# A kernel of bucketed attention and a Mish feed-forward layer: a new table of order and engine behind the beginning of the program

## The chip, the cores and the metric

The kernel runs on one core of a Trainium2 chip. The metric is the device time of one execution in microseconds (us). A core has five engines that each work through their own instructions in order: TensorE (PE, with the weight loads PEld shown apart), VectorE (DVE), ScalarE (ACT), GpSimd (POOL) and SyncE (SP), which here issues the DMA transfers. An engine waits for another through semaphores.

## What is computed

Four batches of eight heads with 768 positions and 64 features go through attention that is masked by hash buckets; then 3072 tokens of 512 features go through a feed-forward layer with Mish, h x tanh(softplus(h)). Inputs are float32, the two weight matrices float64.

```python
q_bits = (np.einsum('bhsd,dk->bhsk', q, proj) > 0).astype(np.int64)
k_bits = (np.einsum('bhsd,dk->bhsk', k, proj) > 0).astype(np.int64)
...
mask = q_bucket[:, :, :, None] == k_bucket[:, :, None, :]
scores = scale * np.matmul(q, k.transpose(0, 1, 3, 2))
scores = np.where(mask, scores, -1000000000.0)
scores = scores - np.max(scores, axis=-1, keepdims=True)
attn = np.exp(scores)
attn = attn / (np.sum(attn, axis=-1, keepdims=True) + 1e-09)
return np.matmul(attn, v).astype(np.float32)
...
h = x @ w_in
sp = np.where(h > 20.0, h, np.log1p(np.exp(np.minimum(h, 20.0))))
g = h * np.tanh(sp)
return (g @ w_out).astype(np.float32)
```

## The kernel before

The function `lsh_attention_mish_ffn` does not issue work as it goes. It builds a plan of 2809 operations, numbered from 0 in the order of the algorithm. An operation (class `Plan`, method `op`) has a name, what it reads and writes, and one or more alternatives: an engine, an estimated duration and a function that issues its instructions. At the end `Plan.ordered` walks through the text `ORDER` and issues each operation where its number stands there. A letter behind the number takes an alternative other than the first (b the second, and so on). So the table fixes two things: the order of instructions on every engine, SP's transfers included, and, for operations with alternatives, the engine. Work is issued in that order under a manual schedule; the framework adds the semaphore waits that the order and the data need.

The program has these parts, all of which overlap in the table:

- *Preparation.* Weights arrive as float64 words and are joined to float32 by integer work (`w_u`, `w_sign`, `w_low`, `w_join`), measured by a sum of squares (`square` on ACT or `gram` on PE), scaled by a power of two and split into two float16 parts (`w_hi`, `w_lo`). q, k and v are split in the same manner. The power of two comes from `stat`: `st` (two small matmuls on PE into columns of the bank ps_t), `half` (DVE reads that), `pw` (DVE or POOL).
- *Attention front*, 96 steps, S0 to S95. A step is two heads by 128 queries. S is eight matmuls into ps_s (768 columns per head, of 512 and 256); from step 13 on there is only one ps_s, so that S waits for both exps of the step before. `max` (DVE, L870) reduces it, `scl` (L876 to L882; DVE in two forms, or POOL) makes the scale and bias, two `exp` (ACT, L895) write the buffer pb and the row sums.
- *Attention back.* `sums`, `rv` (L919), then for each head `hi` (float16 of p times 1/sum: ACT, POOL or DVE; L390, L388, L391), `lo` (what is left: DVE L406, or two instructions on POOL, L412 and L413) and a transposing DMA (`ptturn`, L423) into PT.
- *V*, 48 of them (L951, 36 matmuls each), writes half of the bank ps_t: even ones columns 0 to 255, odd ones columns 256 to 511, which `st` and the hash matmuls `hp` use too. `x_hi` (ACT, L957) and `x_lo` (DVE, L960) read it into X.
- *Feed-forward*, 96 steps. H (24 matmuls, L982 to L984) writes one of two banks, `mish` (ACT, L1000) reads it, `g_hi` and `g_lo` split the result, and O (six matmuls, L1020 to L1022, for each half s of the tokens) accumulates over g. `ob` (ACT or DVE) scales the sum, and a DMA stores it. H8 to H15 need the whole X of the second group of queries, that is V4 to V7.

Mish and exp need different tables on ACT, so that each change between them loads one (ACT_TABLE_LOAD).

The operations that the later text speaks of, with their numbers: S14 558, its max 559, scl 560 and exps 561, 562; S15 599 (scl 601), S16 641 (max 642, scl 643, exps 644, 645), S17 657; V6 646, V7 678; `st` 581, `half` 582, `pw` 583, `w_hi` 584 and 534; x_lo 648 and 680; `lo` 633 on POOL; O30 596; H8 689.

The lines that turn the table into a program, and the alternatives of `scl`:

```python
for w in ORDER.split():
    n, a = (int(w[:-1]), "abcd".index(w[-1])) if w[-1].isalpha() else (int(w), 0)
    o = self.ops[n]
    assert all(q in done for q in o.preds), o.name
    done.add(o)
    yield o.alts[a][2]
...
op("scl", [("DVE", 410, port(lambda: scale(nc.vector, both))), ("DVE", 515, lambda: scale(nc.vector, single)),
           ("POOL", 380, lambda: scale(nc.gpsimd, both))],
```

Of the kernel before, what the change touches and what calls it, by code (L numbers as in the profile page):

```python
# [87 lines left out]
185 14 1 0 71 3 15 107 7 5 6 13 72 42 73 74 134 4b 22 2 16 25 81 26 27 43b 17 76 23 45 8 78 44 77 82 9 48 10 11 24  # L88
12 18 46 49b 19 83 47 20 21 58b 31 84 50 88 51 33 59 85 86 52 87 53 60 108b 56 54 57 110 90 61 55 34 113 146c 109
111 79 126 114b 147b 112 75 89 35 91 115 32b 97 148b 116 123c 80 36 37 118 69 117 28 39 119 29 38 197b 125 124 121  # L90
40 30b 149 41 62 67b 129 63 122 68 92 120 65 93 64 130 94b 66 167 198b 135b 95 70 168 131c 150 136b 132 133 137 199b
98 180 138 159d 169c 160 96 161c 170 200 158 162 163 201 250b 165 164 139 171 251b 181 157 172c 232 209 144 252b 140
208 151 182c 142 166 202 152 210 145b 153 183 173 233 99 174 100 175 211 102 103 101 141 234c 176 186b 143 104 253
184 212 187c 224c 195b 154b 213 127 177 188 155b 214b 225 178 189 226 156 235 245 179 228 215b 196 261 236 229 355
217 190 279b 274 246 227 218 280b 305b 237d 191 105b 230 216 203 263 106 281b 231 193 204 192 238 275 205b 247c 239b
206b 194 240 241 219 254 248 128 276c 207 242 427 249 243 262 266c 306b 220 244 277 255 267 256 300 257 268 221 222
258b 282 223 307b 270 283 269 308 278 271 272b 301 309 292c 259b 329 316 293 310 294 311 302c 312 273 260 334b 318
296 303 317 335b 330 297 264 319 304 295b 320 313 321c 356 331c 298 336b 265 299 314 332 284 322 428 285 286 337 323
290 291 388b 287b 315 338 288b 325 389b 357 326 333 324 383 347d 346 348 339 358c 349 327 390b 351 328 372 289 359
345 361b 352 391 360 362b 384 340 392 400 350 409 375d 363b 376 353 385c 393 377 354 364 414b 379 365 399 373 415b  # L100
341 386 410 380 394 387 378b 366 416b 374 452 401d 411c 395 381 402 417 382 367 403 457b 405 426 412 396b 368 458
# [12 lines left out]
740 707c 673 726 759c 674 676 675 709 677 757 760 724 761 710 785 792 783b 763b 762 725 906 786 779b 787b 764 708c
788 794 765 789 780 766 793 743 803b 1018 711 744 813 712 714 804 795 713 715 745 770 746 814 747b 748 798 805 771b
815c 907 750 772 816 767 807 818 751 801c 910 802 817 806c 819 834c 749 835 1017 808 784 768 845 1019 836 809 769
796b 812 838b 846 810 799 820 752 811 821 753 847b 755 754 839 849 797 842 837b 848 822 923 756 823 800 824 840 825b
865 856 911 827 868 908c 828 857 858b 924 851 869 841 914 873 859c 843 854b 870c 852 855 850 871 912 853 874 860 844
909 861 872 864 862 826 913 903 829 894c 918 863 875 866 895 830 876 896b 927 919 967 920 898 921 877 902 878 922
879 831 880c 944 889 832 882 897 833 946 936c 904 900b 937 899 938 931 947 925b 883 948 959 940 867 949 901 926 950  # L120
890 945 915 939c 941 951c 881c 932 942b 962 952 928 933 891 960 963 968 884 943 961 885 964 953c 965 969 981 970 955
916 982 887 956 917 954c 966 957 987d 958 999 983 985 984 988 971b 886 989 1020 888 934 1000 972b 990b 929b 1001b
991 1002 1024 930 992 1003 974 1021 1028 993 975 1012 1025 1029 1022 994 973 892b 1037 1004b 1204 1158 1005 1030b
# [24 lines left out]
1520b 1577b 1488 1562 1530 1586 1475 1521c 1587 1531 1494 1532 1578 1508 1523 1588 1476 1580 1477 1620 1589c 1533
1590 1550c 1571 1524 1600 1621 1623 1591 1622 1581 1563 1543 1601 1522b 1579 1652 1602b 1960 1593 1603 1564 1594
# [1027 lines left out]
```

## Time and profile before

| | |
|---|---|
| median of 3 runs | 849.79 us (849.61 to 850.22) |
| the profiled execution | 849.03 us, its span 847.3 us |
| PE, busy share of the span | 92% (779.9 us) |
| DVE | 79% (665.4 us) |
| ACT | 72% (612.8 us) |
| POOL | 29% (248.1 us) |
| DMA queue of the kernel, share of 16 engines | 84.8% |

The span runs from the first to the last instruction; the rest of the profiled time lies around it. Busy shares are averages over stages with different limits. In a row of a group stand line, engine, operation, out<-in with shapes and count, then busy us and mean ns of one, then the idle time of the engine just before them and what ended it. In a row of the timeline stand the start, the duration, the engine, the line, and in brackets the idle time before it with its releaser. In a row that gives one tile's instructions stand the shortest, median and longest duration in ns.

### The profile page before, as it was taken

How to read it: one execution, taken by the hardware profiler on the slowest of the kernel's cores; microseconds unless marked ns; L12 is line 12 of the kernel's file. 1: busy time of each engine (PE TensorE's matmuls, PEld its weight loads, DVE VectorE, ACT ScalarE, POOL GpSimd, SP SyncE). 2: the span in 40 equal slices, each digit the busy share in tenths (PEclk: the TensorE clock that was granted, in tenths of full speed). 3: DMA queues.
4: the chain of work that ended last, by engine and by line, in shares of the span. 5: the costliest groups of instructions: out<-in, count | busy, mean ns of one | idle time of the engine just before them, and what ended most of it. 6: DMA issues, size and time to landing. Idle time of an engine off the chain costs nothing. (4 is left out here: it accounts for less than half of the span.)

```text
span 847.3 us, 17219 instructions
## 1 busy us (share of the span) xinstructions
PE 779.9 (92%) x6630; PEld 537.1 (63%) x6630; DVE 665.4 (79%) x1292; ACT 612.8 (72%) x939; POOL 248.1 (29%) x289
## 2 busy tenths in 40 slices
PE   5555768899999999999999999999999999999998
PEld 4333545577667666666666676676677677666764
DVE  6979899888889898888798867789888877767311
ACT  6878899798778667667878867697778765577221
POOL 3546543313231420234311352221213223322000
PEclk9868699999999999999999999999999999999999
DMA  9899999699999978899998878999997785575300
GB/s 312 221 218 237 270 232 223 137 212 212 237 194 197 180 144 162 150 160 234 155 215 167 157 146 138 187 150 210 189 170 135 144 150 101 100 125 107 69 26 26
DMA packets 426547, 144.02 MB, mean 170 GB/s; under 512 B 395744, under 2 KB 416224, under 8 KB 426464
## 3 DMA queue, kind: packets, MB, share of 16 engines
q1 hardware_dynamic: 426464, 142.91, 84.8%
q8 instruction: 52, 0.85, 0.4%
q14 instruction: 31, 0.25, 0.1%
HBM read 36.70 MB, written 7.34 MB: 52 GB/s over the span
## 5 line engine op out<-in xcount | busy, mean ns | idle before, releaser
L895 ACT ACTIVATE pb<-ps_s,svb 128x768 f32<-128x768 f32 x192 | 188.7, 986 | 62.9 <-DVE svb L882 38.5
L982 PE MATMUL ps_acc<-X,wi 128*128 128x256 f16 x768 | 210.1, 274 | 0.5 <-ACT ffb L1000 0.5
L983 PE MATMUL ps_acc<-X,wi 128*128 128x256 f16 x768 | 210.0, 273 | 0.0
L984 PE MATMUL ps_acc<-X,wi 128*128 128x256 f16 x768 | 209.9, 273 | 0.0
L870 DVE TENSOR_REDUCE svb<-ps_s 128x2 f32<-128x1536 f32 x96 | 168.4, 1754 | 43.6 <-PE ps_s L864 41.1
L406 DVE SCALAR_TENSOR_TENSOR hl<-pb,svb,hl 128x768 f16<-128x768 f32 x161 | 164.9, 1030 | 12.7 <-ACT hl L390 8.3
L864 PE MATMUL ps_s<-KT,QT 128*128 128x512 f16 (+1 forms) x768 | 148.4, 338 | 21.1 <-ACT pb L895 16.0
L1022 PE MATMUL ps_o<-wo,ffb 128*128 128x512 f16 x384 | 145.5, 379 | 1.4 <-DVE ffb L406 1.4
L1020 PE MATMUL ps_o<-wo,ffb 128*128 128x512 f16 x384 | 145.6, 379 | 0.0
L1021 PE MATMUL ps_o<-wo,ffb 128*128 128x512 f16 x384 | 145.5, 379 | 0.0
L864 PEld LDWEIGHTS <-QT 128*128 128x128 f16 x768 | 75.1, 100 | 75.8 <-issue 30.4
L951 PE MATMUL ps_t<-PT,VT 128*64 128x256 f16 x1728 | 107.2, 281 | 2.8 <-DVE ho L477 2.0
L951 PEld LDWEIGHTS <-VT 128*64 128x64 f16 x1728 | 94.9, 113 | 17.2 <-issue 15.7
L390 ACT ACTIVATE hl<-pb,svb 128x768 f16<-128x768 f32 x83 | 76.4, 930 | 33.0 <-DMA PT<-hl 15.4
L406 DVE SCALAR_TENSOR_TENSOR ffb<-ffb,smalls 128x512 f16<-128x512 f32 x96 | 72.0, 758 | 35.0 <-POOL ffb L388 27.0
L983 PEld LDWEIGHTS <-wi 128*128 128x128 f16 x768 | 75.3, 98 | 14.9 <-issue 0.5
L982 PEld LDWEIGHTS <-wi 128*128 128x128 f16 x768 | 75.3, 98 | 13.4 <-issue 1.6
L388 POOL TENSOR_SCALAR hl<-pb,svb 128x768 f16<-128x768 f32 x45 | 43.2, 961 | 136.8 <-DVE svb L919 85.2
L984 PEld LDWEIGHTS <-wi 128*128 128x128 f16 x768 | 75.4, 98 | 9.0
L895 ACT ACT_TABLE_LOAD x43 | 55.2, 1283 | 34.2 <-DVE svb L880 20.4
L1000 ACT ACTIVATE ffb<-ps_acc,smalls 128x512 f32<-128x512 f32 x96 | 62.9, 684 | 21.8 <-PE ps_acc L984 15.5
L412 POOL TENSOR_SCALAR pb<-pb,svb 128x768 f32<-128x768 f32 x31 | 30.6, 987 | 138.5 <-ACT hl L390 56.9
(176 smaller groups left out, 990.0 us busy)
## 6 DMA issues: line engine op xcount, KB each, us to landing
out_dram<-ffb SPq DMA_DIRECT2D x24, 256.0 KB, 2.8
stg<-in_k_dram SPq DMA_DIRECT2D x12, 384.0 KB, 4.0
stg<-in_v_dram SPq DMA_DIRECT2D x12, 384.0 KB, 4.2
stg<-in_q_dram SPq DMA_DIRECT2D x9, 512.0 KB, 4.9
wi<-in_moe_w_in_dram SPq DMA_DIRECT2D x7, 512.0 KB, 4.7
wo<-in_moe_w_in_dram SPq DMA_DIRECT2D x6, 512.0 KB, 7.1
stg<-in_moe_w_out_dram SPq DMA_DIRECT2D x6, 512.0 KB, 4.4
PT<-hl SPq DMA_TRANSPOSE x192, 4.0
```

Of the source, the lines that this page charges most:

```text
L390: ACT=lambda: nc.scalar.activation(dst, src, AF.Copy, scale=sc),
L406: return [("DVE", 215 + 1.035 * n, port(lambda: nc.vector.scalar_tensor_tensor(out=dst, in0=src, scalar=sc, in1=hi, op0=ALU.mult, op1=ALU. ...
L864: nc.tensor.matmul(sc[:, hh * S + c0 * P:hh * S + c1 * P], QTb[:, u % 2, sl, qi], KTb[:, j, sl, hh * NCH + c0:hh * NCH + c1].rearrange("p ...
L870: op("max", [("DVE", 1790, lambda: nc.vector.tensor_reduce(out=sv[:, 0], in_=sc.rearrange("p (h e) -> p h e", h=2), axis=AX.X, op=ALU.max, ...
L895: EXP[n, hh] = op("exp", [("ACT", 1075, lambda hh=hh, t=t: nc.scalar.activation(pb[:, t], sc[:, hh * S:(hh + 1) * S], AF.Exp, bias=sv[:, 2 ...
L951: nc.tensor.matmul(pv[hh * D:(hh + 1) * D, 0:256], vt[:, w, hh * NCH + c], pt[:, hh, a * NCH + c].rearrange("p s t -> p (s t)"), start=(x ...
L982: nc.tensor.matmul(o, wh, X[:, 0, c], start=(c == 0), stop=False)
L983: nc.tensor.matmul(o, wh, X[:, 1, c], start=False, stop=False)
L984: nc.tensor.matmul(o, wl, X[:, 0, c], start=False, stop=(c == NCC - 1))
L1020: nc.tensor.matmul(PS[f"o{s}"], gh, wo[:, g, 0, f2], start=first, stop=False)
L1021: nc.tensor.matmul(PS[f"o{s}"], gh, wo[:, g, 1, f2], start=False, stop=False)
L1022: nc.tensor.matmul(PS[f"o{s}"], gl, wo[:, g, 0, f2], start=False, stop=last)
```

## The change

Only the text `ORDER` is replaced. The same 2809 numbers stand in it, in another order and partly with other letters. The first lines of the table differ only in how the engines' operations are interleaved. The rest of the source is unchanged. Of the diff these are the first lines, and those around the operations named above:

```diff
-185 14 1 0 71 3 15 107 7 5 6 13 72 42 73 74 134 4b 22 2 16 25 81 26 27 43b 17 76 23 45 8 78 44 77 82 9 48 10 11 24
+185 14 1 0 71 3 15 107 7 5 6 13 72 42 134 73 4b 22 2 74 25 81 26 27 43b 16 23 45 8 17 44 76 82 9 78 48 10 11 24 77
 12 18 46 49b 19 83 47 20 21 58b 31 84 50 88 51 33 59 85 86 52 87 53 60 108b 56 54 57 110 90 61 55 34 113 146c 109
...
-508 436 527b 477 513 490 523b 514 524 528c 525 515 437 481 483 529 558 538d 467 537 503 536 487 547 433c 484b 539
-516 563b 485 517 530 504 438 559 505b 551 488 506b 540b 541 564 560c 542 548 555 552 507 543 561 439 640 565c 440
-518 544 556 562 557 566 531 576b 599 586d 532 489 575 567 545 533b 587 577b 600 588 568 520 534 589 569 601b 519
-549b 590 602 592 591 603 535 629c 641 593 570b 630 550 571b 546 573 578b 572 594 631 579 574 491 595 632 633b 492
-642 580 553b 581 646 582 615b 635 634 643c 583 554 584b 636 604c 637 585 645 596 644 605 649 657 606c 650 607 651
-678 653b 658 614 608 647 679 648 652 680 659 654 609 689 610 638b 661 611b 612c 660 613 681c 697 690 619c 616b 620
...
+508 436 527b 477 513 490 523b 514 524 528c 525 437 515 481 483 529 558 538d 467 503 487 547 537 433c 484b 536 539
+640 516 563b 485 517 530 504 438 439 551 505b 559 488 548 540b 506b 564 541 560 555 542 552 561 565c 543 507 519 440
+489 562 566 556 599 586c 576b 557 575 544 531 567 532 587 545 600 533b 577b 588 568 546 549b 569 534c 589 518 601
+570b 590 602 592 591 603 535 571b 641 593 550 629c 578b 630 572 595 573 631 579 574 520 491 633b 642 580 632 581 594
+492 553b 582 643 583b 634 646 635 584b 554 645 636 585 644 637 604c 649c 615b 657 605 647 650 606c 651 648 678 607
+653b 658 614 608 596 679 680 659b 609 689 610 661 611 612c 660 613 619b 693 616 690 620 621c 622 617c 662 652 618
...
```

More of the change, by code (lines that the diff above doesn't have):

```diff
@@ L92 @@
[L92 to L101, printed above, removed]
+111 126 114b 147b 112 89 35 91 115 79 32b 97 148b 116 123c 36 37 118 75 117 28 39 119 29 38 197b 125 80 124 121 69
@@ L114 @@
[L114 to L123, printed above, removed]
@@ new lines @@
+1358 1342 1295 1322 1359 1377 1347c 1362 1389 1378 1379 1350 1273 1380b 1363 1312 1351 1390 1364b 1421 1365b 1349
+1391b 1304c 1392 1382 1343 1425 1367 1393 1383 1308b 1410d 1411 1305 1412 1309 1429 1368 1381 1414 1422 1442 1430
+1415 1426 1413c 1321 1366 1431 1445c 1433 1384 1434 1446 1385 1552 1423c 1432 1416 1353 1396 1417 1447d 1369 1397
+1457 1370 1371 1372 1448 1373 1450 1449b 1352 1458 1443 1463 1398 1438 1399 1459b 1400 1453 1401b 1460 1454 1403
+1374 1451 1462 1495 1402c 1452 1461 1424 1439 1478 1479 1404 1489 1496 1354 1490 1435 1498b 1605 1418 1491c 1480b
@@ new lines @@
+1787 1750c 1788 1778 1719 1777c 1779 1780b 1789 1767 1806 1819 1807 1808b 1809 1781 1810 1842 1820 1811b 1821 1812
+1822 1838 1751 1813 1823 1843 1824b 1825 1635 1814 1846 1801 1741 1815 1826 1768 1847 1839 1855 1754b 1848 1827c
+1849 1828 1755 1783 1829 1837 1850 1859 1992 1862b 1830 1863 1840c 1831 1864b 1872 1865 1851 1873 1874b 1866 1875
+1804 1867 1876 1782 1852 1877 1966 1841 1888 1878 1844c 1868 1784 1856 1889 1869 1967b 1894 1879 1890b 1860 1853b
+1881 1891 1816 1880c 1882 1854 1920 1802 1861 1803 1883 1892 1845 1895 1884 1897d 1969b 1817 1898 1906 1900 1899
@@ new lines @@
+1832 1907 1924 1857b 1908b 1901 1909 1858 1902 1910 1870 1903 1833 1904 1921 1929 1942 1930 1911c 1925 1912 1931
+1871 1913c 1932 1915 1934 1896 1916 1914c 1933 1917 1945c 1922b 1955 1946 1947b 1886 1970 1956 1948 1893 1918 1957b
+1949 1885 1958 1923 1950 1959 1887 1951 1943 1968 1926 2026 1971 1987 1976 1952 1972 1993 1977 1944 1973 1974 2007
+1978 1988 1834 1989b 1938 2008 1980 1990 2009 1981 1991 1935 1994 1905 1975 1995 1996 2010b 1997c 2021 2011 1999
+1979 1919 2012 1982 2000 1939 2022 2053 1983 1936c 2023b 2014 2024 2057 1927 2015 2013c 1937 2025 2237 1998c 1953
@@ new lines @@
+2016 2042c 2028 2017 2061 2054 1954 2062 2029 2001 2074 2058 2002 2043 2063b 2044c 2064 2045c 2030 1985 2031 2046
+2003 2032b 2004 2006 2047 2065 2077 2078 2079c 2075 1984 2005 2033c 2048 2089 2095 2035b 2080 2066 2082 2090 2049
+2081 2091b 2055 2036 2092 2070 2083 2056 2093 1818 2076 2084 1940b 2110b 2111 1986 1941 2094 2085 2067 2121 2112c
+2086 2114 2127 2071 2068 2122 2059b 2115 2180 2128 2123b 2130b 2129 2125 2131 2060 2037 2018 2113c 2116 2124 2050
+2117 2132c 2034 2133 2134c 2141 2051 2072 2038 2019b 2147 2096 2136b 2176 2142 2097 2143b 2137 2135c 2144 2087 2039
@@ new lines @@
+2269 2262 2270b 2272 2157 2288 2158 2200 2228 2271 2260c 2160 2285 2263 2239 2292 2264 2240 2159 2196 2241b 2289
+2229 2242c 2161 2273b 2293 2297 2274 2294c 2276 2275b 2286b 2279 2231 2295 2374 2277 2301 2244 2278 2296 2245 2243
+2308d 2230 2255 2309 2310 2287 2280 2318 2256b 2298 2251 2319 2302 2422 2265 2320b 2290c 2281 2321 2291 2467 2370
+2299c 2312 2303b 2311c 2322 2314 2282 2246 2323d 2305 2266 2324 2304 2325 2247 2166 2300 2423 2327b 2334 2313 2371
+2187 2317 2335 2315 2332 2328 2336c 2338 2424 2384 2425 2205 2426b 2326c 2248 2249 2329 2250 2337 2316 2427c 2306
@@ new lines @@
+2330 2307 2352 2468 2343b 2344 2346 2340 2353 2345 2354 2366 2347 2355 2349 2348 2356 2357b 2375 2358 2350 2367
+2359c 2361b 2331 2376 2341 2333 2372b 2342 2377c 2362 2351 2360b 2378 2363 2380 2429 2379 2368c 2430 2391d 2369 2339
+2381 2392 2394b 2364 2401 2397b 2385 2365 2428 2402 2382b 2388 2386 2403b 2393c 2404 2395 2399 2387 2396 2431 2405
+2400 2432 2398 2406b 2373 2417 2407 2408 2283 2437 2389 2418 2410b 2409 2419b 2414 2438 2420 2383 2411 2412 2415
+2421 2390 2440 2436 2441 2434 2439 2442 2451 2444b 2470 2452 2445 2453c 2454 2474 2413 2455 2471 2456b 2443c 2478
@@ new lines @@
+2446b 2475 2416 2479 2483 2433 2480 2469 2481 2457 2458c 2460 2487 2472c 2461 2482 2459c 2473 2484 2476c 2447 2462
+2504 2494c 2464 2488 2267 2505 2463 2552 2495 2506b 2477 2507 2496c 2498 2491 2497c 2465 2500 2508 2466 2448 2501
+2553 2509b 2510 2520 2499 2511 2556 2521 2492 2435 2513 2566 2560 2522b 2514 2512b 2449b 2523 2485 2515 2503 2489
+2516 2524 2502 2529b 2486 2530 2493 2538 2554b 2531c 2526 2539 2540b 2574 2533 2541 2532c 2534 2542 2535 2517 2543
+2536 2544 2490 2561 2545c 2567 2518 2562 2557 2519 2563 2546c 2564 2570 2547 2549 2548 2558c 2565 2555 2525 2550
@@ new lines @@
+2527 2587 2568c 2577b 2578 2579c 2537 2580 2588 2581b 2575 2551 2528 2589b 2585 2559 2582 2591 2576 2609 2590 2592d
+2583b 2603 2610 2571 2611 2600 2604 2639 2593 2605 2594c 2606 2596 2643 2595c 2597 2598 2607 2572c 2584 2612c 2569
+2640 2623 2613 2599 2586 2615 2624 2644 2652 2641c 2625b 2614c 2626 2573 2602 2616 2618 2617 2627 2601 2628 2629
+2619 2620 2630 2645c 2653 2632b 2647 2450 2656 2648 2631 2633 2634 2721 2649b 2635 2642 2650 2608 2651 2636 2657
+2663b 2621b 2664 2646 2673 2722 2695 2665 2674 2675 2660 2637b 2676 2666c 2667 2729 2668 2677 2678b 2669 2689 2679
@@ L205 @@
+2775 2785b 2788 2786 2777 2789 2790 2795 2793 2794 2796 2797 2799 2801 2798 2803b 2802 2804 2800 2805 2806b 2807
+2808
 """
```

150 lines of the change are left out of this document (64 added, 86 removed).

## Prediction

> **What bounds the kernel now.** I began with the span and then cut it into stretches by the engines' busy times, because a new order can only win where PE (TensorE) waits.
>
> ```profile
> span 847.3 us, 17219 instructions
> ```
>
> ```profile
> 136.00:170.00 34.00, 26.86 (x213) 16.77 (x212) 30.91 (x54) 29.01 (x47) 11.56 (x14) 1.00 0.78 165
> 170.00:843.30 673.30, 670.72 (x5655) 460.59 (x5653) 518.23 (x1019) 471.25 (x733) 171.22 (x187) 1.00 0.82 155
> ```
>
> The columns are the stretch, its length, then busy time of PE, PEld, DVE, ACT and POOL, the granted clock, the DMA share and GB/s. From 136 to 170 us PE is busy 26.86 of 34.00, while DVE has 30.91 and ACT 29.01: there DVE and ACT set the pace. From 170 us on PE idles 2.58 of 673.30, at clock 1.00, and DVE (77%) and ACT (70%) have room. A matmul's end is modelled, so I checked that busy PE by its pitch, in the groups of PE from 169.4 us to 843.3 us and in a piece of the timeline.
>
> ```profile
> L982 PE MATMUL ps_acc<-X,wi 128*128 128x256 f16 x721 | 196.6, 273 | 0.0
> ...
> L1020 PE MATMUL ps_o<-wo,ffb 128*128 128x512 f16 x368 | 139.6, 379 | 0.0
> ...
> L864 PE MATMUL ps_s<-KT,QT 128*128 128x512 f16 (+1 forms) x616 | 112.7, 326 | 0.9 <-ACT pb L895 0.9
> L951 PE MATMUL ps_t<-PT,VT 128*64 128x256 f16 x1440 | 85.5, 274 | 0.6 <-ACT X L957 0.3 <-DVE smalls L477 0.2
> L698 PE MATMUL ps_t<-pj,KT 128*128 128x12 f16 x144 | 5.4, 168 | 0.0
> ```
>
> ```profile
> 402.33 0.38 PE L1020 MATMUL ps_o<-wo,ffb 128*128 128x512 f16 x1
> ...
> 404.06 0.38 PE L1022 MATMUL ps_o<-wo,ffb 128*128 128x512 f16 x1
> ...
> 405.67 2.16 PE L951 MATMUL ps_t<-PT,VT 128*64 128x256 f16 x36
> 407.76 0.28 PE L982 MATMUL ps_acc<-X,wi 128*128 128x256 f16 x1
> ...
> 412.90 0.27 PE L984 MATMUL ps_acc<-X,wi 128*128 128x256 f16 x1
> ```
>
> Eight steps from 402.33 to 404.06 are 0.216 us per 512 columns; 47 steps from 407.76 to 412.90 are 0.109 per 256; 36 matmuls of V take 2.09. So H (24 matmuls) is 2.62 us, O (6) 1.30, S (four of each width) 1.30. The stretch holds 3 x 721 x 0.109 = 235.8, 3 x 368 x 0.216 = 238.5, 616/8 x 1.30 = 100.1 and 1440/36 x 2.09 = 83.6, together 658.0, and about 10.5 for the hash matmuls (5.4 in the last row, about as much for the other operand) and statistics. Of its 673.9 us some 5 are waits. **No order can win more than about 5 us after 170 us**, and the one stretch with more in it is 136 to 170.
>
> **The change, part by part.** I decoded both tables: every number is an operation of the plan and its letter the alternative. The lists of the five engines agree up to the 120th ACT, 184th DVE, 64th POOL and 83rd PE operation, which run at 130 to 136 us. What came before stays where it was. No operation is added or removed; behind that point 323 of them change engine and many their place.
>
> *Load.* hi goes from 83/64/45 on ACT/DVE/POOL to 94/63/35, g_hi from 33/26/37 to 42/29/25, lo from 161/31 on DVE/POOL to 156/36, scl from 76/20 to 72/24. With the rows at the end of this part, ACT gains 11 x 0.93 + 9 x 0.72 = 16.7 us and some small copies, about 18 in all; DVE loses 5 lo, about 5. ACT then has 471 + 18 of 673: still under PE. The new table changes 89 times between exp and Mish, the old one 87 times: two more loads at 1.28 us (row of the table load below). I cost the load at nothing because ACT's spare 202 us hide it; without that cover it would be up to 20 us.
>
> *Stretch 136 to 170, first half.* Here the rows are those of POOL, ACT, DVE and PE in order of time.
>
> ```profile
> 133.54 0.69 POOL L876 TENSOR_SCALAR svb<-svb,smalls 128x2 f32<-128x2 f32 x1
> 134.31 0.74 POOL L882 TENSOR_TENSOR svb<-svb 128x2 f32<-128x2 f32 x1
> ```
> ```profile
> 135.10 1.28 ACT L895 ACT_TABLE_LOAD   x1
> 136.40 0.99 ACT L895 ACTIVATE pb<-ps_s,svb 128x768 f32<-128x768 f32 x1
> ```
> ```profile
> 145.17 1.14 PE L864 MATMUL ps_s<-KT,QT 128*128 128x512 f16 x6 [1.41 <-ACT pb L895]
> ...
> 150.83 2.16 PE L951 MATMUL ps_t<-PT,VT 128*64 128x256 f16 x36
> ...
> 157.49 1.46 PE L864 MATMUL ps_s<-KT,QT 128*128 128x512 f16 x8 [0.19 <-ACT pb L895]
> ...
> 162.97 0.27 PE L982 MATMUL ps_acc<-X,wi 128*128 128x256 f16 x1
> ```
> ```profile
> 149.23 1.75 DVE L870 TENSOR_REDUCE svb<-ps_s 128x2 f32<-128x1536 f32 x1
> 153.06 0.16 DVE L477 TENSOR_SCALAR ho<-ps_t 128x1 int32<-128x1 int32 x1 [2.07 <-PE ps_t L951]
> 153.16 1.02 DVE L406 SCALAR_TENSOR_TENSOR hl<-pb,svb,hl 128x768 f16<-128x768 f32 x1
> 154.10 0.15 DVE L462 TENSOR_SCALAR smalls<-ho 128x1 int32<-128x1 int32 x1
> ```
> ```profile
> 154.34 1.15 ACT L390 ACTIVATE wo<-stg,smalls 128x1024 f16<-128x1024 f32 x1 [2.50 <-DVE smalls L462]
> 155.40 0.97 ACT L895 ACTIVATE pb<-ps_s,svb 128x768 f32<-128x768 f32 x1
> ```
>
> The new table gives the scl of S14 (560) to DVE in place of POOL, which took 1.5 us (133.54 to 135.05): the exps of S14 start about 0.4 earlier, and x_hi leaves the place between them (0.4 more), so S15 comes about 0.8 earlier. DVE then pays: it takes scl (0.4) and w_hi 534 (0.66 from POOL) ahead of the exps of S15, so they start about 0.65 later and S16 moves from 145.17 to 145.8. This half loses 0.65.
>
> *Second half.* In the old table the half 582 (the DVE row at 153.06) stands behind V6 (646); in the new one ahead of it. The row shows what that costs: it reads the statistic's columns of ps_t, which PE finished before 150.83, and still waited 2.07 us to the end of V6, which writes other columns of the same bank. Behind it stood pw 583 (154.10), w_hi 584 on ACT (waited 2.50) and behind that, in ACT's order, both exps of S16. In the new order, on my count with the same durations: max of S16 from 149.75 to 151.5, x_lo, half at 151.9, scl 152.4, pw 583 on POOL (now behind a lo that ends at 151.9) 152.3, w_hi 584 from 152.35, exps from 153.4 to 155.35, S17 at 155.75 in place of 157.49. V7 must now wait for x_lo 648 (157.8), and takes its place at 157.9; O30 fills what was PE's wait for x_lo 680; H8 starts at about 161.35, not 162.97. **Gain 1.6 us.** From there the same PE work follows in both tables, so it reaches the end if nothing later is late.
>
> The Trainium skill (PSUM — Partial Sum Buffer, "PSUM bank collisions raise a hardware error") wants PSUM guarded by bank and quadrant, not by address; the 2.07 us row agrees. With a guard by address the half would never have waited and the sum would have the 0.65 loss alone. The same rule says that each half, hash sum or x_lo that stands behind a V in the table waits for that V.
>
> *After 170 us.* PE's order is nearly the old one: mostly an O matmul group changes places with an S. The tight loop is from one S to the next (one ps_s): S, max, scl, two exps.
>
> ```profile
> L870 DVE TENSOR_REDUCE svb<-ps_s 128x2 f32<-128x1536 f32 x96 | 168.4, 1754 | 43.6 <-PE ps_s L864 41.1 <-PE ps_t L474 1.2 <-ACT X L957 0.4
> ...
> L876 DVE TENSOR_SCALAR svb<-svb,smalls 128x1 f32<-128x1 f32 (+1 forms) x111 | 22.5, 229 | 1.8
> ...
> L882 DVE TENSOR_TENSOR svb<-svb 128x2 f32<-128x2 f32 x41 | 6.6, 161 | 1.4
> ```
> ```profile
> L895 ACT ACTIVATE pb<-ps_s,svb 128x768 f32<-128x768 f32 x192 | 188.7, 986 | 62.9 <-DVE svb L882 38.5 <-DVE svb L880 14.5 <-DVE hl L406 3.6
> ...
> L390 ACT ACTIVATE hl<-pb,svb 128x768 f16<-128x768 f32 x83 | 76.4, 930 | 33.0 <-DMA PT<-hl 15.4 <-DVE svb L919 10.8 <-ACT pb L895 3.1
> ...
> L895 ACT ACT_TABLE_LOAD x43 | 55.2, 1283 | 34.2 <-DVE svb L880 20.4 <-DVE svb L882 11.6 <-DVE svb L919 0.9
> ...
> L390 ACT ACTIVATE ffb<-ffb,smalls 128x512 f16<-128x512 f32 x33 | 23.6, 715 | 2.7 <-PE ps_o L1021 2.5
> ```
> ```profile
> L412 POOL TENSOR_SCALAR pb<-pb,svb x31: 905/908/1679, 68.0 to 765.9; 128x768 f32<-128x768 f32 x31
> L413 POOL TENSOR_TENSOR hl<-pb,hl x31: 1638/1644/2048, 69.2 to 766.9; 128x768 f16<-128x768 f32 x31
> ...
> L876 POOL TENSOR_SCALAR svb<-svb,smalls x20: 295/316/1295, 28.2 to 593.1; 128x2 f32<-128x2 f32 x20
> L882 POOL TENSOR_TENSOR svb<-svb x20: 195/196/1187, 28.6 to 593.5; 128x2 f32<-128x2 f32 x20
> ```
>
> The loop is 1.46 + 1.75 + 0.39 + 2 x 0.99 + 0.19 = 5.8 us, and 7.1 where a Mish stands before it, since the load waits for scl too. I summed the PE work between each S and the next in both tables and took the loop off, with what the table puts between its steps. From S18 on no loop is short in the new table; nine had less than 0.4 us to spare before, 13 have now. PE's waits there, about 5 us, should grow a little; bounds are -5 (none left) and +10 (every tight loop late by one DVE lo, 1.03, or thereabouts). I take +0.8, near the old rows since the order is near the old one.
>
> **Sum.** -1.6 + 0.8 = -0.8 us. The profiled execution took 849.03 us (span 847.3); it becomes 848.2. The median of the runs, 849.79, is 0.76 above the profiled one, so I forecast 849.0. What follows the last matmul is the same in kind: an ob half on DVE, then one on ACT, and the store.
>
> **Rivals.** *Cleaner tail (846.2).* The new order also drops half of the 5 us of waits: -1.6 - 2.0. For it: DVE and POOL carry less. Against it: more tight loops.
>
> *POOL in front of scl (853.5, slower).* In the new table 9 of the 24 scl on POOL stand directly behind a POOL lo, before 5 of 20. A lo is 0.91 + 1.64 = 2.55 us in the median, 3.7 when both parts are at their maxima, and then scl follows with 0.5 (2.5 at most). It decides from the point where lo starts later than 2.55 us before max ends; then scl, both exps and the next S are late by up to 1.2 us beyond the loop's spare. Nine places at 0.5 each, the middle of that, give +4.5 on the sum's -0.8. Against it: the medians, and that the old table's S waited only 0.9 us in all behind 170 us (row L864 above).
>
> The Trainium skill (SBUF — State Buffer, "SBUF: two separate sides") calls the SBUF port that DVE and POOL share an exclusive lock, which blocks the second comer whole. The maxima of the POOL rows, about twice the median or more, agree with such blocking; by that rule moving lo to POOL is a loss twice, here part of this rival.
>
> *The first half's loss stays (851.2).* If half 582 is no earlier, because DVE is full there (30.91 of 34.00), S17 keeps +0.65 and the tail +0.8.
>
> **How the numbers follow.** Forecast 0.45, its own range 847.3 to 850.7; cleaner tail 0.25; POOL 0.20; loss kept 0.10. About 0.2%, 1.7 us, is what a measurement can tell from no change. Faster: 0.25 and a quarter of the forecast's share (0.11), 0.36; slower: 0.20 and 0.04 of the last, 0.24; within: 0.40. The range 845.5 to 854.0 takes in the cleaner tail with 0.7 to spare and the POOL case, and leaves out the ends of both, waits all gone or ten of them.
>
> **What would show it.** Right: the half's wait of 2.07 for L951 gone near 152; S17 near 155.8 and H8 near 161.4; PE idle from there to the last matmul within 2 to 4 us; ACT busy about 630, DVE about 660, table loads 44 and 45. Wrong: H8 at 163 or later; PE waiting on L895 by several us after 170, released by a POOL L882; or a clock under 1.00 behind 170 us.

## The result and the profile after

| | before | after |
|---|---|---|
| median | 849.70 us (848.25 to 850.22, 4 runs) | **856.43 us** (855.64 to 857.71, 4 runs) |
| ratio | | 1.0085, 95% interval 1.0071 to 1.0100 |
| the profiled execution | 849.03 us | 856.53 us |

The change makes the kernel slower by 0.85%, some 6.7 us, and the time lies above the predicted range. First the span, from the page of the changed kernel (every line number after is one higher than before).

```profile
span 854.5 us, 17235 instructions
```

Then the stretch from 170 us to the last matmul (columns as in the prediction: length, then busy PE, PEld, DVE, ACT, POOL).

```profile
170.00:850.40 680.40, 672.05 (x5665) 461.86 (x5663) 512.23 (x1026) 490.68 (x759) 181.66 (x190) 1.00 0.81 154
```

PE now idles 8.35 of 680.40 us there, against 2.58 of 673.30 before; the clock is 1.00 as it was. DVE has less to do than before and ACT more, as counted, and both still have a quarter of the time free. So the loss is no overload but 6 us of new waits. The groups of PE in that stretch (the last part is idle time ahead of them and its releaser) say at whose instructions:

```profile
L983 PE MATMUL ps_acc<-X,wi 128*128 128x256 f16 x720 | 196.3, 273 | 1.0 <-ACT ffb L1001 1.0
...
L1023 PE MATMUL ps_o<-wo,ffb 128*128 128x512 f16 x368 | 139.4, 379 | 1.2 <-DVE ffb L407 1.2
...
L865 PE MATMUL ps_s<-KT,QT 128*128 128x512 f16 x311 | 109.5, 379 | 4.3 <-ACT pb L896 4.3
L952 PE MATMUL ps_t<-PT,VT 128*64 128x256 f16 x1440 | 85.5, 274 | 0.2 <-ACT X L958 0.2
...
L699 PE MATMUL ps_t<-pj,KT 128*128 128x12 f16 x144 | 5.4, 168 | 1.2 <-DVE X L961 1.2
```

S waits 4.3 us for exps instead of 0.9, and three groups that hardly waited now wait a microsecond each: H for a Mish, O for a `g_lo`, the hash matmuls for an `x_lo`. A releaser of this view is the last link only. The links in front of it stand in the timeline. Here are its rows at seven of these places.

```profile
204.11 0.16 DVE L478 TENSOR_SCALAR smalls<-ps_t 128x2 int32<-128x2 int32 x1 [2.83 <-PE ps_t L952]
204.19 1.75 DVE L871 TENSOR_REDUCE svb<-ps_s 128x2 f32<-128x1536 f32 x1
...
207.31 1.28 ACT L896 ACT_TABLE_LOAD   x1 [1.83 <-DVE svb L881]
...
211.09 1.14 PE L865 MATMUL ps_s<-KT,QT 128*128 128x512 f16 x6 [1.73 <-ACT pb L896]
...
277.34 0.47 ACT L958 ACTIVATE X<-ps_t,smalls 128x256 f16<-128x256 f32 x1 [2.27 <-PE ps_t L952]
277.83 1.28 ACT L896 ACT_TABLE_LOAD   x1
...
281.24 1.46 PE L865 MATMUL ps_s<-KT,QT 128*128 128x512 f16 x8 [1.21 <-ACT pb L896]
...
414.87 1.01 DVE L407 SCALAR_TENSOR_TENSOR VT<-stg,smalls,VT 128x768 f16<-128x768 f32 x1
415.80 0.48 DVE L961 SCALAR_TENSOR_TENSOR X<-ps_t,smalls,X 128x256 f16<-128x256 f32 x1
416.33 0.44 PE L699 MATMUL ps_t<-pj,KT 128*128 128x12 f16 x12 [1.15 <-DVE X L961]
...
519.35 0.47 ACT L958 ACTIVATE X<-ps_t,smalls 128x256 f16<-128x256 f32 x1 [1.28 <-PE ps_t L952]
...
646.29 0.36 DVE L703 TENSOR_REDUCE hsum<-ps_t 128x96 f32<-128x192 f32 x1 [1.20 <-PE ps_t L952]
...
646.77 1.64 POOL L414 TENSOR_TENSOR hl<-pb,hl 128x768 f16<-128x768 f32 x1
646.82 1.61 DVE L463 TENSOR_SCALAR smalls<-smalls 128x4 int32<-128x4 f32 x1
...
650.99 1.74 POOL L877 TENSOR_SCALAR svb<-svb,smalls 128x2 f32<-128x2 f32 x1 [2.58 <-DVE smalls L478]
...
651.20 0.27 PE L983 MATMUL ps_acc<-X,wi 128*128 128x256 f16 x1 [0.95 <-ACT ffb L1001]
...
652.81 0.81 POOL L883 TENSOR_TENSOR svb<-svb 128x2 f32<-128x2 f32 x1
...
655.76 1.46 PE L865 MATMUL ps_s<-KT,QT 128*128 128x512 f16 x8 [0.48 <-ACT pb L896]
...
805.33 0.48 DVE L961 SCALAR_TENSOR_TENSOR X<-ps_t,smalls,X 128x256 f16<-128x256 f32 x1 [8.57 <-ACT X L958]
805.73 0.74 DVE L407 SCALAR_TENSOR_TENSOR ffb<-ffb,smalls 128x512 f16<-128x512 f32 x1
806.53 0.39 PE L1023 MATMUL ps_o<-wo,ffb 128*128 128x512 f16 x1 [1.21 <-DVE ffb L407]
```

The first four rows show how such a chain is read. DVE is to read a statistic from ps_t (half 746) and stands still for 2.83 us until V8 (L952), which writes other columns of that bank, has ended. Behind the half in DVE's order stands the `max` of S21, whose scores have long been there; behind that a `k_lo` (1.01 us) and scl, on ACT the table load and two exps, and S22 needs them. The matmuls of the statistic stand directly before V8 on PE, so the half never had a chance. In each of the other groups of rows, too, a read of ps_t stands at the head of the chain: x_hi 1042 on ACT ahead of the load for the exps that S31 needs; x_lo 1571 on DVE behind other `lo`s, with hash matmul hp 1473 waiting to write; x_hi 1860 ahead of the exps for S63; hash sum 2247 behind V36, with the `g_lo` for H71's Mish further back; x_lo 2739 ahead of g_lo 2736, which O870 needs.

At H71 and S79 more comes together. Between hash sum 2247 and that `g_lo` DVE has `xf` 2166, whose second step (the row at 646.82) took 1.61 us beside the second instruction of `lo` 2327 on POOL and ended with it; in the kernels "six reads first" and "three V later" below it ended before that `lo` began, and took 0.17. The stretched `xf` (1.44 us) and the hash sum's wait (1.20) are each longer than what H71 waits, and no run parts the two. DVE then ends the `max` for S79 late, and the scl on POOL takes 2.6 us itself. This scl did not queue behind the `lo`, which had ended at 648.41; it waited 2.58 us for DVE.

A read behind a V is not a loss by itself. The table before also has x_hi 1042 behind V13, hash sum 2247 behind V36 and x_lo 2739 behind V47, and the hash sum waited there as long:

```profile
640.78 0.36 DVE L702 TENSOR_REDUCE hsum<-ps_t 128x96 f32<-128x192 f32 x1 [1.26 <-PE ps_t L951]
```

But PE lost nothing by these three: x_hi 1042 stood behind S31's own exps, not ahead of those of S30, which S31 waits for; the `g_lo` for H71's Mish stood right behind hash sum 2247, with no `xf` between them; and O870 started 14 us after V47 had ended, not right behind it. The new table changed what stands behind such a read, and how soon PE needs it.

To put a size on each I took the distance between the starts of neighbouring matmul groups and subtracted the pitch (0.109, 0.216 us per matmul and so on, as in the prediction). The busy time of the windows hides a little of it, because a matmul's end is modelled. In us:

| PE waits at | after | what is late |
|---|---|---|
| S22 | 1.89 | half 746 behind V8 |
| S31 | 1.37 | x_hi 1042 behind V13 |
| hp 1473 | 1.32 | x_lo 1571, late on DVE |
| S63 | 0.71 | x_hi 1860 behind V29 |
| st 2030 | 0.55 | hash sum 2002 behind V32 |
| H71 | 1.09 | hash sum 2247 behind V36, `xf` 2166 beside a POOL `lo` |
| S79 | 0.65 | the same two, then scl 2336 on POOL, 1.74 + 0.81 us |
| O870 | 1.38 | x_lo 2739 ahead of g_lo 2736 |
| four others | 1.13 | |
| together | 10.1 (before: 4.05) | |

At the start, the rows of the changed kernel that answer to those of the stretch from 136 to 170 us:

```profile
114.65 0.37 PE L983 MATMUL ps_acc<-X,wi 128*128 128x256 f16 x1
...
153.28 0.15 DVE L478 TENSOR_SCALAR ho<-ps_t 128x1 int32<-128x1 int32 x1
...
153.94 1.02 DVE L407 SCALAR_TENSOR_TENSOR hl<-pb,svb,hl 128x768 f16<-128x768 f32 x1
...
157.36 1.46 PE L865 MATMUL ps_s<-KT,QT 128*128 128x512 f16 x8
...
159.85 0.27 PE L952 MATMUL ps_t<-PT,VT 128*64 128x256 f16 x1 [1.02 <-DMA PT<-hl]
160.93 2.15 PE L952 MATMUL ps_t<-PT,VT 128*64 128x256 f16 x35 [0.81 <-DMA PT<-hl]
...
164.37 0.27 PE L983 MATMUL ps_acc<-X,wi 128*128 128x256 f16 x1
...
849.09 0.38 PE L1021 MATMUL ps_o<-wo,ffb 128*128 128x512 f16 x1
```

The same for before: H0's first matmul and that of the last O group.

```profile
113.04 0.38 PE L982 MATMUL ps_acc<-X,wi 128*128 128x256 f16 x1
...
841.79 0.38 PE L1020 MATMUL ps_o<-wo,ffb 128*128 128x512 f16 x1
```

From H0 to H8 it is 49.72 us (before 49.93), from H8 to the last O group 684.72 (before 841.79 - 162.97 = 678.82). H0 itself came 1.61 late, ahead of all changed orders. It is the tail that lost 5.9.

### The profile page after: what moved, and what is told of

It reads as the page before. It is cut to its first block, busy times and chain, and to the rows that moved or that the text cites. A ratio compares the mean times of both kernels' runs of the same rounds, so it can differ in the third digit from the quotient of the medians.

```text
span 854.5 us, 17235 instructions
## 1 busy us (share of the span) xinstructions
PE 782.1 (92%) x6630; PEld 538.3 (63%) x6630; DVE 659.7 (77%) x1301; ACT 631.3 (74%) x964; POOL 255.3 (30%) x285
## 5 line engine op out<-in xcount | busy, mean ns | idle before, releaser
L865 PE MATMUL ps_s<-KT,QT 128*128 128x512 f16 (+1 forms) x768 | 150.5, 342 | 24.1 <-ACT pb L896 19.4
L407 DVE SCALAR_TENSOR_TENSOR hl<-pb,svb,hl 128x768 f16<-128x768 f32 x156 | 159.4, 1027 | 13.3 <-ACT hl L391 6.6
L952 PE MATMUL ps_t<-PT,VT 128*64 128x256 f16 x1728 | 105.8, 278 | 6.2 <-DMA PT<-hl 3.4
L391 ACT ACTIVATE hl<-pb,svb 128x768 f16<-128x768 f32 x94 | 86.2, 929 | 32.0 <-DMA PT<-hl 16.4
L952 PEld LDWEIGHTS <-VT 128*64 128x64 f16 x1728 | 93.5, 112 | 20.0 <-issue 16.0
L413 POOL TENSOR_SCALAR pb<-pb,svb 128x768 f32<-128x768 f32 x36 | 37.0, 1027 | 154.7 <-ACT hl L391 97.0
L389 POOL TENSOR_SCALAR hl<-pb,svb 128x768 f16<-128x768 f32 x35 | 34.0, 971 | 132.5 <-DVE svb L920 70.4
```

What stands on the lines that cost most here:

```text
L391: ACT=lambda: nc.scalar.activation(dst, src, AF.Copy, scale=sc),
L407: return [("DVE", 215 + 1.035 * n, port(lambda: nc.vector.scalar_tensor_tensor(out=dst, in0=src, scalar=sc, in1=hi, op0=ALU.mult, op1=ALU. ...
L865: nc.tensor.matmul(sc[:, hh * S + c0 * P:hh * S + c1 * P], QTb[:, u % 2, sl, qi], KTb[:, j, sl, hh * NCH + c0:hh * NCH + c1].rearrange("p ...
L952: nc.tensor.matmul(pv[hh * D:(hh + 1) * D, 0:256], vt[:, w, hh * NCH + c], pt[:, hh, a * NCH + c].rearrange("p s t -> p (s t)"), start=(x ...
```

## The experiments

Two theories. The **bank theory**: in the tail, reads of ps_t (`half`, hash sum, `x_hi`, `x_lo`) stand behind a V or late on their engine, and PE pays for it. The **rivals**: the start loses; the new work on POOL ahead of scl is slow (the prediction's rival); the new orders and engines cost something all over. "Tail" is the distance from H8's first matmul to the first of the last O group in the profiled execution. It leaves out when H0 starts, which varied from 112.7 to 114.7 us between these executions. Ratios are to the table before, run beside each kernel on the same chip. In the variants the lines stand two or three lower than in the kernels before and after, for the table is shorter: V is L949, S L862, an exp L893.

| kernel | median us | ratio (95%) | tail us |
|---|---|---|---|
| before | 849.70 | | 678.82 |
| after | 856.43 | 1.0085 (1.0071 to 1.0100) | 684.72 |
| new table again | 856.13 | 1.0084 (1.0065 to 1.0104) | 684.27 |
| old start, new tail | 857.39 | 1.0094 (1.0081 to 1.0108) | 685.72 |
| new start, old tail | 848.79 | 1.0002 (0.9987 to 1.0017) | 677.65 |
| half 746 first | 854.25 | 1.0062 (1.0048 to 1.0076) | 683.95 |
| old table, V8 first | 853.14 | 1.0045 (1.0032 to 1.0057) | 681.50 |
| six reads first | 854.44 | 1.0076 (1.0064 to 1.0088) | 683.23 |
| seven scl off POOL | 854.37 | 1.0071 (1.0059 to 1.0083) | 684.13 |
| both | 853.09 | 1.0056 (1.0041 to 1.0071) | 681.60 |
| three V later | 856.57 | 1.0091 (1.0073 to 1.0110) | 684.81 |
| all repairs, V8 later | 852.67 | 1.0047 (1.0029 to 1.0065) | 681.46 |
| four moves | 851.82 | 1.0035 (1.0022 to 1.0049) | 680.11 |
| all repairs, V8 kept | 849.09 | 1.0001 (0.9992 to 1.0010) | 677.28 |
| old table, halves first | 848.70 | 1.0003 (0.9995 to 1.0012) | 680.13 |
| new start, old tail, early reads | 847.25, 846.85 | 0.9983 (0.9969 to 0.9997), 0.9974 (0.9963 to 0.9985) | 675.71, 675.59 |

### Which part of the table

The old table up to H8 (operation 689) and the new one behind it, and the other way round; what the first part has already issued is left out of the second.

> The old table up to and with H8 (689), then what is left in the order and with the engines of the new table. Theory T (the loss of the new table, about 7 us, sits in single waits of PE behind 170 us, about 6 us of them): 855 to 856, +5.5 to +6.5 on before, with the same waits ahead of S22, S31, H71 and O870. Rival S (the start, where H0 came 1.6 us late in the profile of the new table): 851 or less.

> The new table up to and with H8 (689), then what is left in the order and with the engines of the old one. Theory T: the start of the new table is worth nothing on balance (S17 earlier, then V7 waits for its transposed tiles): 849 to 850.5. Rival S: 851 or more. The forecast's own step (-1.6 at H8): 848.

The whole loss goes with the tail: 857.39 us with the old start, 848.79 with the old tail. The new start is worth nothing that these runs can tell.

### One read, moved in both tables

In the new table half 746 is set ahead of V8, in the old one V8 ahead of the half. One number moves; the order of every engine stays.

```diff
 new table
-745 798 746
+745 746 798
 old table
-746 814 747b 748 798
+798 746
```

> The new table with one number moved: half 746 is issued ahead of V8 (798) and no longer behind it; every engine's own order stays. Theory B (a read of the bank ps_t waits for the PE write that stands last ahead of it in the table, other columns or not): the half's wait of 2.83 us goes, S22 comes about 1.9 us earlier, V8 about 0.3 later, in all -1.6 on the new table: about 854.8. Rival (S22 waits because k_lo stands between max and scl): S22 no earlier, 856.4.

> The old table with one number moved: V8 (798) is issued ahead of half 746; every engine's own order stays. Theory B: half 746 waits for V8's end (about 204.0 for 200.6), max 814 behind it on DVE is 3.3 us later, the loop has 1.2 to spare, S22 about 2 us late: +2 on before, 851.8. Rival (the wait goes by columns): no change, 849.7.

The timeline of the new table with the half first, and then that of the old one with V8 first:

```profile
201.03 0.16 DVE L475 TENSOR_SCALAR smalls<-ps_t 128x2 int32<-128x2 int32 x1 [0.72 <-PE ps_t L472]
...
201.25 2.16 PE L949 MATMUL ps_t<-PT,VT 128*64 128x256 f16 x36 [0.25 <-DVE smalls L475]
```
```profile
205.80 0.16 DVE L475 TENSOR_SCALAR smalls<-ps_t 128x2 int32<-128x2 int32 x1 [4.00 <-PE ps_t L949]
...
211.30 0.92 PE L862 MATMUL ps_s<-KT,QT 128*128 128x512 f16 x5 [1.55 <-ACT pb L893]
```

The half now waits for the statistic's own matmul (L472), V8 is 0.25 us late in its place, and S22's wait is gone. Not all of it reaches the end: S28, further on, waits 1.24 us where it had waited 0.51, and the tail is 0.8 us shorter (0.3 against the new table's second run), less than the median's 2.2. In the old table the moved V8 brings the same wait, and S22's wait with it (1.7 us): 4.0 us of 849.15, twice the forecast, 2.7 of them in the tail, where hp 752 and st 877 now wait 0.7 and 1.4 us as well. Both directions with one number: the wait comes from where a read stands against a V, although it reads other columns.

### Six reads ahead of their V

Half 746, x_hi 1042, x_hi 1860, hash sums 2002 and 2247, x_hi 2738 and x_lo 2739, each set ahead of the V behind which it stood, with what must come before it; all engine orders kept.

```diff
-2001 2074 2058 2002
+2001 2002 2074 2058
...
-2737 2746 2738 2739
+2737 2738 2739 2746
```

> The new table with six groups of reads of ps_t set ahead of the V that they stood behind (half 746 ahead of V8, x_hi 1042 ahead of V13, hi 1879 and x_hi 1860 ahead of V29, hsum 2002 ahead of V32, rv 2324, g_lo 2304 and hsum 2247 ahead of V36, x_hi 2738 and x_lo 2739 ahead of V47). Each engine's own order of instructions is that of the new table to the last one, and no operation changes engine. Bank theory: the waits at S22 (1.89), S31 (1.37), S63 (0.71), st 2030 (0.55), H71 (1.09) and O870 (1.38), 7.0 us together, go or shrink to a fifth; the whole takes 849.5 to 852. Rival, the new table's engine orders and its changes of engine are themselves slower (POOL ahead of scl, more tight loops): with the orders unchanged, at most half 746's measured 2.2 us come back, 854 to 855.

The forecast fails: 854.44, no better than half 746 alone. The timeline shows why, at V36 and hash sum 2247.

```profile
643.16 0.35 DVE L700 TENSOR_REDUCE hsum<-ps_t 128x96 f32<-128x192 f32 x1
...
643.56 2.15 PE L949 MATMUL ps_t<-PT,VT 128*64 128x256 f16 x36 [1.28 <-DVE hsum L700]
```

A V that stands behind a read waits for it just as the read waited for the V. V13, V29, V32, V36 and V47 now wait 0.66, 1.45, 0.50, 1.28 and 1.15 us, where S31, S63, st 2030, H71 and O870 had waited 1.37, 0.71, 0.55, 1.09 and 1.38. Only at V8 was the read ready almost at once. So the place in the table only chooses who waits. The theory in its second form: there must be PE work between the producer and the next V, and the reader must come early on its own engine.

### POOL in front of scl, alone and with the reads

The letter of seven scl behind a `lo` on POOL (738, 920, 964, 1072, 2336, 2377, 2453) is taken away, which gives them to DVE. The second kernel joins this to the six reads and sets x_lo 1571 directly behind scl 1558.

```diff
-1072c
+1072
...
-2336c
+2336
```

> The new table with seven scl behind 172 us (738, 920, 964, 1072, 2336, 2377, 2453), each directly behind a lo on POOL, given to DVE directly behind their max; nothing else changed, so all reads of ps_t still stand behind their V. POOL rival of the prediction: 0.5 us for each place, 3.5 us, 853.0. Bank theory: only S79 (0.65) and part of S31 (1.37, of which the scl on POOL is the last step) can go, so -0.5 to -1.5: 855 to 856; the waits at S22, H71, O870 stay as they are.

> The edits of the six reads and of the seven scl together, and x_lo 1571 on DVE moved directly behind scl 1558 (hp 1473 waited 1.32 us for it). If the waits seen behind 172 us in the new table's trace are the whole loss, 8 to 9 of its 10 us go: 848 to 849.5, level with the table before. If something else lies in the new tail, it stays above 851.

854.37: the rival is worth about a microsecond, not 3.5, and since the intervals of this kernel and the new table overlap, even that is an estimate. The timeline has scl 2336 on DVE in 0.42 us, where POOL had taken 2.63:

```profile
649.55 0.23 DVE L874 TENSOR_SCALAR svb<-svb,smalls 128x2 f32<-128x2 f32 x1
649.81 0.16 DVE L880 TENSOR_TENSOR svb<-svb 128x2 f32<-128x2 f32 x1
```

S79's wait is gone, while S22, S31, H71 and O870 wait as before. S31 waits as long as ever, though scl 1072, which had started 1.06 us after its `max` because of the POOL `lo` ahead of it, is now on DVE. Together with the reads the time is 853.09, less than hoped, since the V still wait as above.

### PE's order, and one move too many

V8 behind H13, V32 behind O531 with st 2030 after it, V36 behind S78, the three reads ahead of them; first alone, then with all repairs.

```diff
-745 798 746 814 747b 748 750 910
+745 746 814 747b 748 750 910 798
...
-2246 2323d 2305 2266 2324 2304 2325 2247 2166 2300 2423 2327b 2334
+2246 2323d 2266 2324 2304 2325 2247 2166 2300 2423 2327b 2334 2305
```

> The new table with only PE's order changed: V8 behind H13, V32 behind O531 (st 2030 after it), V36 behind S78, and half 746, hsum 2002, hsum 2247 ahead of their V in the text; ACT, DVE and POOL keep the new table's orders to the last instruction. Second form of the bank theory: S22's 1.89, st 2030's 0.55 and H71's 1.09 go and no V waits in their place, -3.0 to -3.5 us against the new table: 853 to 853.5; setting only the reads ahead had turned them into waits of V36 (1.32), V32 (0.55) and V8 (0.29). Rival, the order of ACT and DVE makes these waits whatever PE's order is: no better than with the reads ahead alone, 854 to 855.

> The new table, with the three V that follow a hash or statistic matmul directly on PE set one matmul group later (V8 behind H13, V32 behind O531 with st 2030 after it, V36 behind S78), half 746, hsum 2002 and hsum 2247 ahead of them; and on ACT and DVE x_hi 1860 directly behind exp 1876, x_hi 1042 behind exp 1074, x_lo 1571 directly behind scl 1558, g_lo 2736 ahead of x_lo 2739, and the seven scl off POOL. Bank theory in its second form (one of the two always waits: what counts is that there is PE work between producer and next V, and that the reader comes early on its own engine): the waits at S22, S31, hp 1473, V29 or S63, V32, V36 or H71, O870 all go; from H8 to the last O 678 to 680 us as in the old table, total 848 to 850. If the new tail has another cost that my list of waits doesn't show: above 851.5.

The first gains nothing, 856.57, and misses both its forecasts. V32 and V36 behave (no waits at st 2030, H71 and S79, 0.8 us at V37 in their place). S79's wait is gone although scl 2336 is still on POOL: with hash sum 2247 and `xf` out of the way it ran while DVE stood still, and took 0.30 and 0.19 us.

```profile
649.35 0.30 POOL L874 TENSOR_SCALAR svb<-svb,smalls 128x2 f32<-128x2 f32 x1
649.74 0.19 POOL L880 TENSOR_TENSOR svb<-svb 128x2 f32<-128x2 f32 x1
```

But V8 does not behave:

```profile
202.89 0.27 PE L980 MATMUL ps_acc<-X,wi 128*128 128x256 f16 x1 [1.41 <-ACT ffb L998]
...
205.60 2.16 PE L949 MATMUL ps_t<-PT,VT 128*64 128x256 f16 x36
...
207.69 0.94 ACT L388 ACTIVATE VT<-stg,smalls 128x768 f16<-128x768 f32 x1 [4.85 <-PE ps_t L949]
...
212.62 0.70 PE L862 MATMUL ps_s<-KT,QT 128*128 128x512 f16 x3 [2.17 <-ACT pb L893]
```

V8 had covered PE's wait for H13's Mish; without it H13 stands 1.54 us. And ACT's next operation, the split of v into VT, waits 4.85 us for V8 to leave that buffer, with the exps for S22 behind it (2.33 us). The second kernel has the same two waits: 852.67, over the 851.5 that was to speak for another cost in the tail. The next kernel decides between the two.

### Closing the account

All repairs with V8 left where it was (half 746 ahead of it); and four moves alone, with PE's and POOL's orders as in the new table: x_hi 1860 directly behind exp 1876, x_hi 1042 behind exp 1074, x_lo 1571 directly behind scl 1558, g_lo 2736 ahead of x_lo 2739. The forecasts call these four late readers, but only two of the reads move ahead on their engine (x_hi 1860 and x_lo 1571). x_hi 1042 moves back, behind the two exps that it had held up, and x_lo 2739 moves back by one place, behind the `g_lo` that PE needs.

> The kernel of all repairs, but with V8 back directly behind st 745 (half 746 ahead of it), since H13 in front of V8 waited 1.54 us for mish 795 and S22 then 2.33 us. If the waits listed behind 172 us are the whole loss of the new tail: from H8 to the last O 681.5 - 1.55 - 2.33 + 0.3 = about 678 us, as in the old table (677.7 to 678.8), total 848.5 to 849.5, ratio 1.000 to 1.001. If the new tail has a cost beside them, the stretch stays above 680 us and the total above 851.

> The new table with only four late readers moved on their own engines: x_hi 1042 behind exp 1074 and x_hi 1860 directly behind exp 1876 on ACT, x_lo 1571 directly behind scl 1558 and g_lo 2736 ahead of x_lo 2739 on DVE. PE's and POOL's orders, all engines and the three V behind hash and statistic matmuls stay. If late readers make these waits: hp 1473's 1.37, S63's 0.71, O870's 1.38 and about 0.46 of S31's 1.37 go, 3.9 us in all, 852.3 (852 to 853). If PE's order (a V directly behind its neighbour in the bank) makes them: no more than 1.4 go, 855 or above.

Both come out as expected: 849.09 (ratio 1.0001) and 851.82. First the stretch behind 170 us of the kernel with all repairs, then S and V in its groups, then S of the kernel with the four moves:

```profile
170.00:841.60 671.60, 669.97 (x5655) 460.75 (x5653) 512.94 (x1036) 489.24 (x757) 176.16 (x176) 1.00 0.81 156
```
```profile
L862 PE MATMUL ps_s<-KT,QT 128*128 128x512 f16 x308 | 108.4, 379 | 0.5 <-ACT pb L893 0.5
L949 PE MATMUL ps_t<-PT,VT 128*64 128x256 f16 x1440 | 85.5, 274 | 0.9 <-DVE X L958 0.5 <-DVE smalls L475 0.3 <-ACT X L955 0.2
```
```profile
L862 PE MATMUL ps_s<-KT,QT 128*128 128x512 f16 x308 | 108.4, 379 | 2.6 <-ACT pb L893 2.6
```

PE idles 1.63 us in place of 8.35, with the new table's engines for `hi`, `g_hi` and `lo` untouched (only the seven scl change theirs). So the new tail has no cost beside its waits, and most of POOL's work, 176.16 us for 181.66 in the new table, stayed in it. Of the 7.1 us or so between the new table (1.0084) and all repairs (1.0001), the four moves give about 4.2: the waits at S31, hp 1473, S63 and O870 are gone, and S32 waits 0.6 in their place. The reads and V at half 746, V32 and V36 and the seven scl give the rest, about 2.9.

> The new table itself once more, so that its variants are compared with it on one chip: 856 to 857, ratio 1.0085 as measured.

The new table run beside these variants: 1.0084, as first measured.

### A version under both

In the old table, half 582 ahead of V6, half 2031 ahead of V32, and x_lo 1078 ahead of lo 1131:

> The old table with half 582 set ahead of V6 and half 2031 ahead of V32 (engine orders kept), and x_lo 1078 on DVE moved ahead of lo 1131 (hp 1167 waited 0.92 us for it). If each repaired wait is worth itself: S17 about 1.7 us earlier, hp 1167 0.9: 847.0 to 847.5, faster than before by 0.25%. If V7's transposed tiles set the pace behind S17, as they did in the new table, only the 0.9 is left: 848.5 to 849.

Nothing (1.0003): H8 comes 0.8 us earlier behind H0, but V32 waits 1.21 us for the half, hp 1167 still waits 0.95, and the tail is 1.3 longer. The second was a misreading, as the timeline of the kernel before shows:

```profile
296.93 0.47 ACT L957 ACTIVATE X<-ps_t,smalls 128x256 f16<-128x256 f32 x1
...
297.45 0.54 PE L698 MATMUL ps_t<-pj,QT 128*128 128x12 f16 x16 [0.76 <-ACT X L957]
```

The releaser is x_hi 1125 on ACT, behind two exps. So x_hi 1125 goes ahead of exp 1140, exp 1560 ahead of square 1516, and x_hi 1895 ahead of mish 1921, on the new start and the old tail (numbers of other engines between them left out):

```diff
-1140 1141 1125
+1125 1140 1141
...
-1516 1560
+1560 1516
...
-1921 1895
+1895 1921
```

> The new start with the old tail (848.8 without further edits), and three places of the old tail mended on ACT: x_hi 1125 ahead of exp 1140 (hp 1167 waited 0.92 us for it), exp 1560 ahead of square 1516 (S49 waited 0.44 to 0.74), x_hi 1895 ahead of mish 1921 (V30 waited 0.40). If late readers of ps_t cost what PE waits for them: -1.7, 847.0 to 847.5, under the table before. If the work set aside is late in its turn: no change, 848.5 to 849.

> The kernel with the new start, the old tail and three exps and x_hi mended once more, to firm up a ratio of 0.9983: again 0.997 to 0.9995 if its gain is the 1.7 us of three waits.

847.25 us, and 846.85 in the second run: 0.17% and 0.26% below the table before, with intervals below 1, and 9 us below the changed kernel. Against the same start and tail without the three moves (677.65) the tail is 1.9 us shorter, and the three waits are gone. Behind 170 us PE then idles 0.28 us (second run):

```profile
170.00:841.00 671.00, 670.72 (x5665) 461.21 (x5662) 520.89 (x1020) 472.20 (x734) 169.42 (x187) 1.00 0.82 156
```

## Why the prediction was wrong

- **The step that failed is the tail, "I take +0.8".** It measured +5.9 in the profiled executions, and 6.7 between the means of the new tail (684.72, 684.27, 685.72) and the old (678.82, 677.65). Only the time around the S loop was summed, and of the 9.0 us at the eight named places 4.3 stand at hp, st, H and O, outside that loop. The prediction itself says that "each half, hash sum or x_lo that stands behind a V in the table waits for that V", but no such read behind 170 us was looked for or priced. Four hash or statistic matmuls stand directly before a V on PE behind H8 in the new table (745, 890, 2001, 2246), one in the old (2030). Three of the four make S22, st 2030 and H71 wait; behind 890 PE loses nothing. The other waits come from where a read stands on DVE or ACT, and that has to be read off each engine's order. The argument "near the old rows since the order is near the old one" hid this: an O put on the other side of a V leaves the order near, and the half without its gap.
- **The bound of +10 was right in size, but for another mechanism.** It assumed every tight S loop late by a DVE `lo`. The number of tight loops, 13 against 9, told nothing: the four S that wait most had a bank read (S22, S31, S63) in their loop, or one ahead of it and a POOL scl in it (S79). The cleaner tail came out the other way. One of its reasons was wrong as well: DVE has less to do (659.7 us of the span for 665.4), but POOL has more (255.3 for 248.1).
- **The bank rule was right and only half understood.** The 2.83 us at half 746, the 4.00 in the old table with V8 moved, and V36's 1.28 for a read show that it binds in both directions and follows the table. This agrees with the Trainium skill (PSUM — Partial Sum Buffer, "PSUM bank collisions raise a hardware error") as far as it wants PSUM guarded by bank and quadrant, not by address.
- **First half of the start, 0.65 late at S16: right.** S15 stands 25.22 us behind H0, before 25.83, and S16 32.73, before 32.13: 0.6 earlier and then 0.6 later.
- **Second half of the start, -1.6 at H8: right to S17, then lost.** Half 582's wait for V6 is gone. S17 stands 42.71 us behind H0, before 44.45: 1.74 earlier, as forecast. But V7 did not start when x_lo 648 was through: it waited for transposed tiles until 160.93, 5.97 us after the `lo` at 153.94 ended (154.96), a wait that the prediction didn't name. H8 gained 0.2 in place of 1.6. In the other profiled executions with the new start it is 49.03 to 49.85 us from H0 to H8, with the old start 49.97 and 50.42, so the gain is some 0.1 to 0.9. The kernel with the new start and the old tail shows no gain in its time.
- **POOL in front of scl, 0.20, +4.5 us: POOL did cost PE time, but not in the way that was priced.** Where an scl did queue behind a `lo` (1072), PE's wait stayed when it was taken off POOL. Where an scl on POOL did make PE wait (2336, S79 0.65), its `lo` had long ended, and it was slow itself: 1.74 and 0.81 us, against medians of 0.309 and 0.195. And beside `lo` 2327, new on POOL, DVE's `xf` took 1.61 us in place of 0.17. H71 and S79, behind these operations, wait 1.7 us of the 10.1. Seven scl taken off POOL gave about 0.0013 of the time, 1.1 us. The prediction's "about twice the median or more" for the maxima of the POOL rows does not hold for L413, 2048 for 1644.
- **The load was right.** ACT was busy 631.3 us and DVE 659.7, as forecast (630, 660); neither was a bound, and a kernel with nearly the same letters came out level with the one before (1.0001).

## What to carry to other kernels

Where an order is written by hand, list for every bank its writers and readers in that order, and look for a reader that comes late on its engine, for one that stands ahead of work that PE needs soon, and for a writer that follows its neighbour with no other matmul between: in the last case a place ahead or behind only chooses which of the two waits. Such a reader goes to the front if its data are there and to the back if they are not. Two reads and one exp set to the front on ACT, with the new start and the old tail, came out 1.4 to 2.2 us under the table before. Look also at what runs on POOL beside a small DVE operation in such a chain. Before a matmul group is moved, look for the wait that it covers and the buffer that it holds.

## What was not expected of the hardware

- H0, behind a start whose engine orders are the same in both tables, began between 112.7 and 114.7 us in these executions: two microseconds of scatter, more than most single edits are worth. Distances within the tail (new table: 684.72 and 684.27) repeat better.
- scl 2336 took 0.23 and 0.16 us on DVE and 1.74 and 0.81 on POOL, where the medians are 0.309 and 0.195. On POOL it was slow beside DVE's `lo` and `hi` work, and took 0.30 and 0.19 in the kernel with three V later, where DVE stood still at that moment. `xf` on DVE took 1.61 us beside a POOL `lo` and 0.17 ahead of it. Both point to DVE and POOL holding each other up; no run changes that alone.
